# The second products of a batch pair by seven block products, and split weights kept in DRAM

## The chip, the cores and the metric

The kernel runs on one core of a Trainium2 chip. The metric is the time of one execution on the device in microseconds (us), as the median of several runs; a profile is one further execution, recorded instruction by instruction. The engines are TensorE (PE, matrix products), VectorE (DVE), ScalarE (ACT) and GpSimd (POOL); SyncE (SP) issues nearly all transfers.

## What is computed

Four batches of 448 tokens by 768 channels go through attention with 12 heads, a mixer of low rank and a second mixer. Cut to the two mixers, on which the change bears:

```python
# x: (4, 448, 768) from the attention
u = x + ((x.T @ U) @ V).T                      # first mixer, tokens (rank 32)
x = u + relu(u @ wa1) @ wa2                    # "FFN a": 768 -> 3072 -> 768
u = x + (relu(x.T @ w_tok1) @ w_tok2).T        # second mixer, tokens (256)
out = u + relu(u @ wb1) @ wb2                  # "FFN b": 768 -> 1536 -> 768
```

The inputs are float64. A product in full precision is made of three matmuls on values split into a high and a low part: high by high, low by high, high by low.

## The kernel before

**Layout.** Activations lie as channels by tokens: `xs[i]` is a tile of 128 partitions by 6 blocks of 448, one for each batch of a pair. The weights of an FFN are worked in chunks of 128 hidden channels: FFN a has 24, FFN b 12, taken in groups of `G = 2`. Batches 0 and 1 are the first pair, 2 and 3 the second.

**Order of the work.** Attention of batches 0 and 1 comes first (to about 200 us); then FFN a of the first pair runs while the attention of batches 2 and 3 is woven in (to about 620 us), then the first pair's token mixing and FFN b (to about 1000 us), then both FFNs of the second pair in `pair_ffn`.

**Weights.** In the first pair `load_w` loads a chunk (`w_raw`, 768 KB), turns float64 into float32 on ACT, DVE and POOL (`to_f32`), stores the float32 chunk in DRAM (`cache`, tiles `c_a...` and `c_b...`, line 159) and splits it (`split`, lines 143 to 145: high part on ACT, low part on POOL). In the second pair `again` (line 191) loads the cached float32 chunk and splits it once more.

**First products of the second pair.** In the middle groups (10 of FFN a, 4 of FFN b) the first products of both batches and two chunks are a 2 by 2 block product. `seven` (line 615) makes it by seven block products for eight, from weight sums (`w1_blocks`, line 212) and activation sums (`sums`, line 589). A block product is three channel blocks of three matmuls, 9 matmuls of 448 columns: 63 a group.

**Second products.** `second` (line 651) takes, for each batch and each of the six output blocks, two chunks of three matmuls, 12 x 6 = 72 matmuls a group, and DVE adds each output block from PSUM to `xs` (line 659). Those of one group run beside the first products of the next (`rest_`, line 690).

**What sets the order.** The code gives dependencies and a program order; the framework's scheduler puts the instructions of each engine into a fixed order when the program is built. Each engine then works its list in order and waits where a semaphore isn't reached. So does SP: a transfer that waits for its source holds up the transfers behind it. Tiles come from pools with a fixed number of buffers (`wh` and `wl`, the split chunks, have four each; `pu` five).

## Time and profile before

| | us |
|---|---|
| median of 3 runs (lowest, highest) | 1553.95 (1550.92, 1559.37) |
| the profiled execution | 1552.55 |
| its span, first to last instruction | 1550.8 |
| PE busy in the span | 1462.3 (94%) |
| DVE / ACT / POOL busy | 1100.2 / 710.3 / 814.0 |
| mean granted TensorE clock | 0.982 of full speed |

The chain of work that ended last is PE for 69% of the span, DVE for 9%, POOL for 7%, DMA for 6%. In a row of instructions, `out<-in` names the tiles: `ps_g` and `ps_p` are first products (plain and by blocks), `ps_x` second products, `gs` the split hidden activations. Matmuls are pipelined: the time of one row is longer than the distance to the next.

### The profile page before, as it was taken

The page shows a single profiled execution, that of the slowest core. Times are in us where ns is not written, and L with a number is a line of the kernel's source. Part 1 is how long each engine was busy: PE and PEld are TensorE (multiplying, and loading weights), DVE is VectorE, ACT ScalarE, POOL GpSimd, SP SyncE. Part 2 cuts the span into 40 slices and gives each one's busy share as a digit, 9 for nine tenths or more (in the row PEclk, how much of TensorE's full clock was granted, in tenths as well). Part 3 has the DMA queues.
Part 4 walks back from the last instruction along what each step waited for, and adds up shares of the span by engine and source line. Part 5 has one row for each costly group of instructions (what it writes and reads, how often), then busy time and mean ns, then how long its engine had stood idle before and what let it go on. Part 6 is the DMA issues. An engine that isn't in the chain of part 4 may idle for free.

```text
span 1550.8 us, 21621 instructions
## 1 busy us (share of the span) xinstructions
PE 1462.3 (94%) x7522; PEld 1296.6 (84%) x7522; DVE 1100.2 (71%) x1811; ACT 710.3 (46%) x1413; POOL 814.0 (52%) x839
## 2 busy tenths in 40 slices
PE   4999968899999999999899999889999999999998
PEld 3766657788888899898798999779999999998997
DVE  6888877888887888566858766596756655567753
ACT  4777756566566665343634434342322221333311
POOL 6888967777876655454735553024443523103510
PEclk9999979999999999999999999999999999999999
DMA  6756644656655544451505540421211111201203
GB/s 169 171 133 156 175 140 130 182 151 195 194 175 150 147 125 142 165 178 63 194 31 184 183 153 32 157 68 52 72 52 51 62 58 46 77 18 54 72 21 92
DMA packets 96588, 180.94 MB, mean 117 GB/s; under 512 B 8992, under 2 KB 66304, under 8 KB 96480
## 3 DMA queue, kind: packets, MB, share of 16 engines
q1 hardware_dynamic: 96160, 179.57, 37.7%
q8 instruction: 59, 0.97, 0.3%
q14 instruction: 49, 0.40, 0.1%
q10 hardware_dynamic: 320, 0.00, 0.0%
HBM read 107.19 MB, written 36.57 MB: 93 GB/s over the span
## 4 chain that ended last, share of the span: by engine, by line
PE 69%; DVE 9%; POOL 7%; DMA 6%; issue 4%; ACT 3%; SPq 1%; ACTq 0%; DVEq 0%; POOLq 0%
PE ps_x L79 29%; PE ps_g L79 16%; PE ps_p L79 11%; PE pv L79 3%; PE sc L79 2%; PE pt L362 2%; PE ps_u L79 2%; PE ps_t L79 2%; POOL w_bits L134 2%; POOL p L343 1%; DVE w_bits L126 1%; DMA qr<-in_q_dram 1%; POOL w L145 1%; DMA c_a<-w_bits 1%; POOL sq L256 1%
## 5 line engine op out<-in xcount | busy, mean ns | idle before, releaser
L79 PE MATMUL ps_x<-gs,w 128*128 128x448 f32 x2592 | 575.6, 370 | 13.8 <-DVE xT L544 3.9
L79 PEld LDWEIGHTS ps_x<-gs,w 128*128 128x128 f32 x2592 | 484.1, 190 | 58.6 <-DVE xT L544 7.0
L79 PE MATMUL ps_g<-u,w 128*128 128x448 f32 x1584 | 345.0, 370 | 0.9 <-POOL u L445 0.9
L79 PEld LDWEIGHTS ps_g<-u,w 128*128 128x128 f32 x1584 | 296.7, 189 | 25.5 <-POOL u L445 1.2
L134 POOL TENSOR_TENSOR w_bits<-w_bits,w_round 128x768 uint32<-128x768 uint32 (+3 forms) x80 | 143.5, 1794 | 106.6 <-DVE w_bits L131 45.4
L145 POOL TENSOR_TENSOR w<-w 128x768 fp32r<-128x768 f32 x44 | 87.2, 1988 | 196.8 <-ACT w L144 143.3
L145 POOL TENSOR_TENSOR w<-w_bits,w 128x768 fp32r<-128x768 f32 (+3 forms) x82 | 147.6, 1807 | 78.3 <-ACT w L144 74.6
L659 DVE TENSOR_TENSOR xT<-ps_x,xT 128x448 f32<-128x448 f32 x216 | 130.3, 618 | 78.5 <-PE ps_x L79 77.9
L544 DVE TENSOR_TENSOR xT<-ps_x,xT 128x448 f32<-128x448 f32 x216 | 132.3, 616 | 42.1 <-PE ps_x L79 39.2
L336 ACT ACTIVATE p<-sc,nm 112x448 f32<-112x448 f32 x192 | 121.1, 633 | 56.0 <-DVE nm L334 52.7
L343 POOL TENSOR_SCALAR p<-p,sm 112x448 f32<-112x448 f32 x192 | 133.2, 706 | 19.9 <-DVE sm L340 18.0
L79 PE MATMUL sc<-ks,qs 128*112 128x448 f32 x384 | 120.2, 406 | 23.6 <-DMA ks<-both 12.9
L145 POOL TENSOR_TENSOR w_a<-w_a 128x384 fp32r<-128x384 f32 (+1 forms) x28 | 41.2, 1470 | 186.0 <-DVE w_t L223 171.9
L334 DVE TENSOR_REDUCE nm<-sc 112x1 f32<-112x448 f32 x192 | 116.3, 613 | 23.0 <-PE sc L79 21.8
L362 PEld LDWEIGHTS pt<-ident,p 112*112 112x112 f32 x768 | 89.8, 135 | 37.2 <-issue 10.9
L362 PE MATMUL pt<-ident,p 112*112 112x112 f32 x768 | 111.9, 262 | 4.5 <-POOL p L343 3.7
L126 DVE TENSOR_SCALAR w_bits<-w_bits 128x768 f32<-128x768 f32 (+3 forms) x80 | 76.3, 954 | 47.2 <-ACT w_bits L125 46.7
L630 DVE TENSOR_TENSOR pu<-ps_p,pu 128x448 f32<-128x448 f32 x98 | 58.7, 616 | 67.5 <-PE ps_p L79 67.4
L130 ACT ACTIVATE w_round<-w_raw 128x768 uint32<-128x768 uint32 (+3 forms) x80 | 69.8, 873 | 73.4 <-POOL w_bits L134 69.4
L373 ACT ACTIVATE ph<-pt 112x448 fp32r<-112x448 f32 (+1 forms) x168 | 88.4, 543 | 31.1 <-PE pt L362 30.0
L125 ACT ACTIVATE w_bits<-w_raw 128x768 f32<-128x768 f32 (+3 forms) x80 | 70.1, 877 | 55.1 <-POOL w L145 37.3
L377 DVE TENSOR_TENSOR pl<-pt,ph 112x448 fp32r<-112x448 f32 x144 | 87.2, 613 | 10.4 <-ACT ph L373 9.7
(110 smaller groups left out, 2283.9 us busy)
## 6 DMA issues: line engine op xcount, KB each, us to landing
w_raw<-in_moe_w_ch_dram SPq DMA_DIRECT2D x72, 768.0 KB, 4.4
ks<-both SPq DMA_DIRECT2D x92, 224.0 KB, 3.7
c_a<-w_bits SPq DMA_DIRECT2D x48, 384.0 KB, 3.3
qs<-both SPq DMA_DIRECT2D x96, 112.0 KB, 2.9
w<-c_a SPq DMA_DIRECT2D x28, 384.0 KB, 3.2
c_b<-w_bits SPq DMA_DIRECT2D x24, 384.0 KB, 3.2
w_a<-c_a SPq DMA_DIRECT2D x20, 384.0 KB, 2.9
w<-c_b SPq DMA_DIRECT2D x16, 384.0 KB, 3.1
```

What stands on the lines that cost most here:

```text
L79: nc.tensor.matmul(o, lhsT=l, rhs=r, start=start, stop=stop)
L126: nc.vector.tensor_scalar_max(f(w), f(w), TINY)
L134: nc.gpsimd.tensor_tensor(w, w, r, op=ALU.add)
L145: nc.gpsimd.tensor_sub(lo, w, f(hi))
L334: nc.vector.tensor_reduce(nm, sc, axis=AX.X, op=ALU.max, negate=True)
L336: nc.scalar.activation(p, sc, AF.Exp, bias=nm, accum_out=sm[:, c % 2:c % 2 + 1])
L343: nc.gpsimd.tensor_scalar(x, x, sm[:, i:i + 1], 1.0, op0=ALU.mult, op1=ALU.mult)
L362: nc.tensor.transpose(pt[:, c * CP:(c + 1) * CP], pr[c][:, kc * CP:(kc + 1) * CP], ident[:CP, :CP],)
L373: nc.scalar.activation(ph, pt, AF.Copy)
L377: nc.vector.tensor_sub(pl, pt, f(ph))
L544: nc.vector.tensor_add(xT[:, dc], px, xT[:, dc])
L659: nc.vector.tensor_add(xT[:, dc], px, xT[:, dc])
```

## The change

**Split weights in DRAM.** `load_w` now also stores the high and the low part of each chunk (`parts`, tiles `h_a...` and `h_b...`): two more stores of 384 KB for each of the 72 chunks, on SP's queue. `load_wt` stores the split token-mixing weights in eight smaller stores, and `wt_again` loads them back for the second pair. `again` and `halved` load split parts and split nothing.

**Second products by seven.** `second_of` makes a group's second products as seven block products, 7 x 9 = 63 matmuls, each into a trio (one PSUM tile of three banks, two such tiles, shared with the token mixing). The seven sums are kept over all groups of an FFN: in `xs` itself, in the two `raw` buffers and in the `w` and `r` buffers; DVE adds a trio to its sum in one operation of 1344 columns. `join` puts the seven sums together after the last middle group, on DVE and POOL. The hidden activations are now also needed as four sums (`t1` to `t4` in `seven`), each split on ACT and DVE.

**Weight blocks in a ring.** `w1_ring` and `w2_ring` prepare one block for each of the seven rounds, about four rounds ahead: unchanged blocks come split from DRAM, the four sums of each side are made from the cached float32 chunks on POOL and split on ACT and POOL. Ten transfers of 384 KB a group take the place of four. `pu` has 11 buffers, the pool `wt` closes with the first pair.

Per program, PE has 7350 matmuls for 7476; SP issues 800 transfers for 544, POOL 974 instructions for 844.

The diff, cut to its core:

```diff
@@ load_w
+        if keep:
+            parts[keep] = dram.tile([p, 2, n], F32, name=f"h_{keep}")
+            for i, t in enumerate((hi, lo)):
+                nc.sync.dma_start(parts[keep][:, i], f(t))
         return hi, lo
...
     def again(key):
         hi, lo = slots()
-        nc.sync.dma_start(f(lo), cache[key])
-        split(f(lo), hi, lo)
+        for i, t in enumerate((hi, lo)):
+            nc.sync.dma_start(f(t), parts[key][:, i])
         return hi, lo
...
+    def ring(tag, src):
+        t = wp.tile([P, 2, HD], F32R, tag=tag, bufs=4, name="w_b")
+        if len(src.shape) == 3:
+            nc.sync.dma_start(f(t), src)
+        else:
+            split(src, t[:, 0], t[:, 1])
+        return t[:, 0], t[:, 1]
...
+    def w2_ring(nm, j, a):
+        k0, k1 = [f"{nm}2_{j + i}" for i in range(2)]
+        a["a11"] = ring("wl", parts[k0][:, :, :HD])
+        a11, s3, a12, s1 = staged((k0, k1))
+        yield
+        a["a12"] = ring("wl", parts[k1][:, :, :HD])
+        yield
+        add(s1, s3)
+        sub(s3, a11, s3)
+        sub(a11, s1, a11)
+        sub(a12, a12, a11)
+        a["s4"] = ring("wl", a12)
+        yield
+        a["s1"] = ring("wl", s1)
+        yield
+        a["s3"] = ring("wl", s3)
+        yield
+        a["s2"] = ring("wl", a11)
+        yield
+        a["a22"] = ring("wl", parts[k1][:, :, HD:])
+        yield
...
@@ seven
+            def parted(key, t):
+                s = pools["g"].tile([P, 2, S], F32R, tag="g", name="gs")
+                nc.scalar.activation(s[:, 0], t, AF.Copy)
+                nc.vector.tensor_sub(s[:, 1], t, f(s[:, 0]))
+                gs[key] = s[:, 0], s[:, 1]
...
-            gs[1][0] = relu(plus(product("s", "s4", "b22"), u4))
+            g12 = output(None, product("s4", "b22"), u4)
+            t1 = diff(nc.gpsimd, g12, g11)
+            parted("t1", t1)
+            t3 = diff(nc.gpsimd, g22, g12)
+            parted("t3", t3)
+            t2 = diff(nc.vector, g22, t1)
+            parted("t2", t2)
+            parted("t4", diff(nc.vector, g21, t2))
...
+        def second_of(a, gs, acc, fresh):
+            for key, l, r in (("p1", "a11", "b11"), ("p2", "a12", "b21"), ("p3", "s4", "b22"),
+                              ("p5", "s1", "t1"), ("p7", "s3", "t3"), ("p6", "s2", "t2"),
+                              ("p4", "a22", "t4")):
+                px = trio("ps_x")
+                for c in range(HC):
+                    three(px[c], pick(a[l], c), gs[r], True, True)
+                to = acc[key]
+                for x, ps in zip(to, [trios[-1]] if len(to) == 1 else px):
+                    if fresh and key in ("p1", "p5", "p6", "p7"):
+                        nc.scalar.activation(x, ps, AF.Copy)
+                    else:
+                        nc.vector.tensor_add(x, ps, x)
+                yield
+
+        def join(acc):
+            x1, x6, x5 = acc["p1"][0], acc["p6"][0], acc["p5"][0]
+            c11, c12, c21 = [acc[k][0] for k in ("p2", "p3", "p4")]
+            nc.gpsimd.tensor_add(c11, c11, x1)
+            nc.vector.tensor_add(x6, x6, x1)
+            for c, x7 in enumerate(acc["p7"]):
+                nc.vector.tensor_add(x7, x7, x6[:, c])
+                nc.vector.tensor_add(c21[:, c], c21[:, c], x7)
+            nc.gpsimd.tensor_add(c12, c12, x6)
+            nc.gpsimd.tensor_add(c12, c12, x5)
+            x = pools["tb"].tile([P, HC, S], F32, tag="t3", name="x22")
+            nc.sync.dma_start(x, x22)
+            nc.vector.tensor_add(x5, x5, x)
+            for c, x7 in enumerate(acc["p7"]):
+                nc.vector.tensor_add(x5[:, c], x5[:, c], x7)
...
         for j0 in range(G, n - G, G):
-            a = a or w1_blocks(nm, j0)
-            w2s = [w2_chunk(nm, w2, j0 + i) for i in range(G)]
-            gs = [[None] * 2 for _ in xs]
-            for _ in seven(a, b, gs):
-                if j0 > G:
-                    next(rest_, None)
-                    next(rest_, None)
+            more = j0 + G < n - G
+            gs, a2, a_next = {}, {}, {}
+            it = seven(a, b, gs)
+            for r in range(1, 8):
+                for _ in range(1 if j0 > G else 2):
+                    next(rest_, None)
+                next(it)
+                if r == 4:
+                    prep1 = w1_ring(nm, j0 + G, a_next) if more else last_w1()
+                    prep2 = w2_ring(nm, j0, a2)
+                next(prep1, None)
+                next(prep2, None)
...
-    open_pools(rest, (("xs", 4, 0), ("pu", 5, 0), ("tb", 1, 0)))
+    open_pools(rest, (("xs", 4, 0), ("pu", 11, 0), ("tb", 1, 0), ("M", 2, 1), ("p", 2, 1)))
```

**Where instructions stand now.** First the list of PE in the steady loop of FFN a, second pair, one group: `ps_p` are first products by blocks (`w_a`, `w_s`, later `w_b` are weight blocks, `u` and `t_...` activation blocks), `ps_x` second products. Before:

```order
L79 MATMUL ps_p<-u,w_a 128x448 x16
L79 MATMUL ps_p<-t_11161,w_s 128x448 x9
L79 MATMUL ps_x<-gs,w 128x448 x12
L79 MATMUL ps_p<-t_11162,w_a 128x448 x9
L79 MATMUL ps_x<-gs,w 128x448 x12
L79 MATMUL ps_p<-t_11163,w_a 128x448 x9
L79 MATMUL ps_x<-gs,w 128x448 x12
L79 MATMUL ps_p<-t_11258,w_s 128x448 x9
L79 MATMUL ps_x<-gs,w 128x448 x12
L79 MATMUL ps_p<-u,w_s 128x448 x9
```

After, the same place:

```order
L79 MATMUL ps_p<-u,w_b 128x448 x9
L79 MATMUL ps_x<-gs,w_b 128x448 x9
L79 MATMUL ps_p<-t_11392,w_b 128x448 x9
L79 MATMUL ps_x<-gs,w_b 128x448 x9
L79 MATMUL ps_p<-t_11393,w_b 128x448 x9
L79 MATMUL ps_x<-gs,w_b 128x448 x9
L79 MATMUL ps_p<-t_11481,w_b 128x448 x9
L79 MATMUL ps_x<-gs,w_b 128x448 x9
L79 MATMUL ps_p<-t_11394,w_b 128x448 x9
L79 MATMUL ps_x<-gs,w_b 128x448 x9
```

Blocks of nine alternate, where before twelve second products stood between two first ones.

Second, DVE at the turn from one group to the next in the same loop. Before (line 630 adds a first product, 659 a second one, 513 makes the low part of a hidden activation):

```order
L659 TENSOR_TENSOR xT<-ps_x,xT 128x448 x3
L630 TENSOR_TENSOR pu<-ps_p,pu 128x448
L513 SCALAR_TENSOR_TENSOR gs<-pu,gs 128x448
L630 TENSOR_TENSOR pu<-ps_p,pu 128x448
L659 TENSOR_TENSOR xT<-ps_x,xT 128x448 x2
```

After (line 750 adds a first product, 819 a trio, 768 makes a difference of hidden activations, 756 a low part):

```order
L750 TENSOR_TENSOR pu<-ps_p,pu 128x448
L819 TENSOR_TENSOR X<-ps_x,X 128x1344
L768 TENSOR_TENSOR pu<-pu 128x448
L756 TENSOR_TENSOR gs<-pu,gs 128x448
L768 TENSOR_TENSOR pu<-pu 128x448
L756 TENSOR_TENSOR gs<-pu,gs 128x448
L819 TENSOR_TENSOR xT<-ps_x,xT 128x1344
L756 TENSOR_TENSOR gs<-pu,gs 128x448 x2
L750 TENSOR_TENSOR pu<-ps_p,pu 128x448
```

Behind the add of the group's last first product now come six operations on two SBUF tiles, with one add of a trio among them. POOL's list at the same turn, after (line 145 is the low part of a weight block, 264 and 267 the weight sums, 768 the two differences t1 and t3):

```order
L267 TENSOR_TENSOR w_f<-w_f 128x384 x3
L145 TENSOR_TENSOR w_b<-w_f,w_b 128x384 x4
L768 TENSOR_TENSOR pu<-pu 128x448 x2
L145 TENSOR_TENSOR w_b<-w_f,w_b 128x384 x3
L264 TENSOR_TENSOR w_f<-w_f 128x384
```

The differences stand behind four low parts of weight blocks. Third, SP where the first pair's weights begin to be loaded. Before:

```order
L159 DMA c_a_0_2883<-w_bits 128x768
L116 DMA w_raw<-in_moe_w_ch_dram 128x6x128
L116 DMA w_raw<-in_moe_w_ch_dram 128x768 x2
L159 DMA c_a_1_2899<-w_bits 128x768
L116 DMA w_raw<-in_moe_w_ch_dram 128x6x128
L159 DMA c_a_0_3176<-w_bits 128x768
```

After:

```order
L159 DMA c_a_0_2883<-w_bits 128x768
L169 DMA h_a_0_2889<-w 128x768 x2
L116 DMA w_raw<-in_moe_w_ch_dram 128x6x128
L116 DMA w_raw<-in_moe_w_ch_dram 128x768 x2
L159 DMA c_a_1_2902<-w_bits 128x768
L169 DMA h_a_1_2908<-w 128x768
L116 DMA w_raw<-in_moe_w_ch_dram 128x6x128
L169 DMA h_a_1_2908<-w 128x768
L159 DMA c_a_0_3182<-w_bits 128x768
```

The stores of the high and the low part stand in front of the next chunks' loads.

## Rows read from the trace of the kernel before

**Rows 1.** Busy time by stage; window, its length, then each engine's busy us.

```profile
core 0: us, PE busy (x) PEld busy (x) DVE busy (x) ACT busy (x) POOL busy (x), PEclk, DMA share, GB/s
0.00:200.00 200.00, 162.64 (x886) 119.73 (x886) 155.99 (x318) 134.43 (x361) 160.96 (x303) 0.96 0.64 158
200.00:620.00 420.00, 397.47 (x2127) 352.79 (x2128) 343.32 (x572) 260.47 (x532) 294.62 (x313) 0.97 0.52 159
620.00:930.00 310.00, 297.37 (x1474) 270.21 (x1473) 215.37 (x299) 133.25 (x194) 162.65 (x95) 0.99 0.41 144
930.00:1050.00 120.00, 111.36 (x568) 98.43 (x567) 85.93 (x141) 45.05 (x86) 32.54 (x22) 0.99 0.25 84
1127.09:1281.82 154.73, 154.73 (x765) 143.37 (x765) 93.27 (x150) 40.99 (x70) 60.53 (x43) 1.00 0.17 57
1281.82:1401.90 120.08, 118.32 (x605) 108.85 (x604) 70.11 (x119) 39.38 (x73) 26.34 (x16) 0.99 0.14 48
...
1495.60:1550.80 55.20, 49.59 (x264) 45.23 (x262) 23.36 (x38) 9.51 (x17) 7.71 (x4) 0.98 0.23 70
```

**Rows 2.** Chain that ended last, steady loop; start us, length us, what.

```profile
1127.09 5.07 PE ps_p L79 x25
...
1149.38 2.44 PE ps_x L79 x12
...
1154.45 5.07 PE ps_p L79 x25
```

**Rows 3.** Instruction groups of DVE, 1127 to 1282 us; count, busy us, mean ns, idle before.

```profile
L659 DVE TENSOR_TENSOR xT<-ps_x,xT 128x448 f32<-128x448 f32 x67 | 41.5, 621 | 23.1 <-PE ps_x L79 23.0
L630 DVE TENSOR_TENSOR pu<-ps_p,pu 128x448 f32<-128x448 f32 x39 | 23.7, 617 | 30.6 <-PE ps_p L79 30.6
L513 DVE SCALAR_TENSOR_TENSOR gs<-pu,gs 128x448 fp32r<-128x448 f32 x22 | 17.6, 800 | 4.7 <-ACT gs L512 4.4
```

**Rows 4.** Instruction groups of DVE, 930 to 1127 us, 384 columns from PSUM.

```profile
L439 DVE TENSOR_TENSOR xs<-pt_x,xs 112x384 fp32r<-112x384 f32 x16 | 8.4, 550 | 3.5 <-ACT xs L438 3.4
```

**Rows 5.** Instruction groups of POOL, 1127 to 1282 us.

```profile
L145 POOL TENSOR_TENSOR w_a<-w_a 128x768 fp32r<-128x768 f32 x5 | 9.3, 1854 | 0.0
...
L145 POOL TENSOR_TENSOR w_a<-w_t,w_a 128x384 fp32r<-128x384 f32 x5 | 5.1, 1020 | 5.3 <-ACT w_a L144 5.3
```

**Rows 6.** Timelines of POOL and DVE; start us, length us, instruction.

```profile
1150.47 1.86 POOL L145 TENSOR_TENSOR w_a<-w_a 128x768 fp32r<-128x768 f32 x1
1152.28 2.23 POOL L145 TENSOR_TENSOR w<-w 128x768 fp32r<-128x768 f32 x1
...
1151.40 1.41 DVE L513 SCALAR_TENSOR_TENSOR gs<-pu,gs 128x448 fp32r<-128x448 f32 x1
```

**Rows 7.** One line's instructions over the run; duration ns lowest/median/highest.

```profile
L513 DVE SCALAR_TENSOR_TENSOR gs<-pu,gs x56: 606/626/2179, 1032.4 to 1497.4; 128x448 fp32r<-128x448 f32 x56
```

**Rows 8.** Who PE waited for, 930 us to the end; us, times, longest.

```profile
PE ps_p L79 <- DVE t L598: 2.3, 4, 1.0
PE ps_x L79 <- DVE xT L659: 2.1, 2, 1.7
PE ps_x L79 <- ACT w L144: 1.3, 1, 1.3
```

**Rows 9.** Transfers, 200 to 930 us: queue's packets, MB, share; issues, median us to landing.

```profile
q1 hardware_dynamic: 58537, 110.47, 47.2%
...
c_a<-w_bits SPq DMA_DIRECT2D x48, 384.0 KB, 3.3
```

**Rows 10.** Who ACT waited for, 200 to 930 us.

```profile
ACT both L300 <- DMA qs<-both: 16.3, 7, 5.6
...
ACT w_bits L125 <- DMA c_a<-w_bits: 5.9, 4, 2.3
```

**Rows 11.** Chain that ended last, 200 to 930 us, shares by line.

```profile
by line: PE ps_g L79 25.4%; PE ps_x L79 24.4%; issue 5.0%; PE sc L79 3.7%; PE pt L362 3.4%; PE pv L79 3.3%; POOL w_bits L134 3.3%; DVE w_bits L126 2.7%; POOL w L145 2.6%; DMA c_a<-w_bits 2.5%; DVE w_bits L131 2.0%; PE ps_u L79 1.8%; DVE w_b
```

More of the change, by code (lines that the diff above doesn't have):

```diff
@@ new lines, in w1_blocks, with w1_ring @@
+        sub(a12, a12, a11)
+        split(a12, *res["s4"])
+        return res
+    def ring(tag, src):
[5 more added lines that the diff above has]
+        return t[:, 0], t[:, 1]
+    def w1_ring(nm, j, a):
+        k0, k1 = [f"{nm}1_{j + i}" for i in range(2)]
+        a["a11"] = ring("wh", parts[k0][:, :, :HD])
+        a11, a12, s3, s1 = staged((k0, k1))
+        yield
+        a["a12"] = ring("wh", parts[k0][:, :, HD:])
+        yield
+        add(s1, s3)
+        sub(s3, a11, s3)
+        sub(a11, s1, a11)
+        a["s2"] = ring("wh", a11)
+        yield
+        a["s3"] = ring("wh", s3)
+        yield
+        a["s1"] = ring("wh", s1)
+        yield
+        a["a22"] = ring("wh", parts[k1][:, :, HD:])
+        yield
+        sub(a12, a12, a11)
+        a["s4"] = ring("wh", a12)
+        yield
@@ L474, in rank_steps, with trio @@
             yield
+    trios = []
+    def trio(name):
+        t = pools["M"].tile([P, 3, 512], F32, tag="M", name=name)
+        trios.append(t[:, :, :S])
+        return [t[:, i, :S] for i in range(3)]
     def token_mix(xT, w):
@@ L479, in token_mix @@
         for hf in range(2):
-            pts = [psum("ts"[rc], [P, HALF], "ps_t1") for rc in range(RC)]
+            if trios:
+                pts = [t[:, :HALF] for t in trio("ps_t1")]
+            else:
+                pts = [psum("ts"[rc], [P, HALF], "ps_t1") for rc in range(RC)]
             for c, (xh, xl) in enumerate(to_tokens(xT, hf)):
@@ L573, in ffn, with pair_ffn @@
                         after(i)
-    def pair_ffn(nm, w1, w2, xs, us, a, after, half=None, last=lambda: None, begun=None):
+    def pair_ffn(nm, w1, w2, xs, us, a, after, half=None, last=lambda: None, begun=None,
+                 late=lambda: None):
         n = w1.shape[1] // P
@@ L660, in second @@
-                if done and dc % 3 == 2:
-                    done(dc // 3)
-                yield
-        def seconds(gs, w2s):
-            for xT, g in zip(xs, gs):
-                yield from second(xT, g, w2s)
-        def chunks(j0):
-            return ([w1_chunk(nm, w1, j0 + i) for i in range(G)],
-                    [w2_chunk(nm, w2, j0 + i) for i in range(G)])
+                if dc % 3 == 0:
+                    px = trio("ps_x")
+                for i, (g, w) in enumerate(zip(gs, ws)):
+                    three(px[dc % 3], pick(w, dc), g, i == 0, i == len(gs) - 1)
@@ L698, in pair_ffn, with last_w1 @@
-        drain(rest_)
-        for i in range(2):
-            drain(second(xs[i], [first(us[i], ws) for ws in w1s], w2s,
-                         half and (lambda h: half(i, h))))
-            after(i)
+        prep1, prep2 = iter(()), iter(())
+        x22 = dram.tile([P, HC, S], F32, name=f"x22_{nm}")
+        acc, w1s = None, []
+        def last_w1():
+            for i in range(n - G, n):
+                key, res = f"{nm}1_{i}", []
+                w1s.append(res)
+                for h in range(2):
+                    res.append(ring("wh", parts[key][:, :, h * HD:(h + 1) * HD]))
+                    yield
@@ new lines, in pair_ffn @@
+        w = late()
+        w2s = []
+        gs = []
+        for r in range(1, 8):
+            next(rest_)
+            next(prep2, None)
+            if r in (2, 4):
+                gs.append(first(us[0], w1s[len(gs)]))
+            if r > 3:
+                i = r - 4
+                if i % 2 == 0:
+                    w2s.append([])
+                key = f"{nm}2_{n - G + i // 2}"
+                w2s[-1].append(ring("wl", parts[key][:, :, (i % 2) * HD:(i % 2 + 1) * HD]))
+        join(acc)
@@ L704, in begin @@
+        for i in range(2):
+            if i:
+                gs = [first(us[1], ws) for ws in w1s]
+                last()
+            drain(second(xs[i], gs, w2s, half and (lambda h: half(i, h))))
+            after(i, w)
     def begin(nm, w1, u, beside=iter(())):
```

206 lines of the change are left out of this document (138 added, 68 removed).

## The prediction, made before the changed kernel was run

> **What bounds the kernel now.** I read the profile by stages first. The table of stages [rows 1] gives for each stretch how long PE was busy and at which granted clock. Before 200 us PE idles a fifth of the time (attention alone). From 200 to 930 us, the first pair of batches, it idles 22.5 + 12.6 = 35 us. From 930 us on, the second pair, it idles only 8.6 + 1.8 + 5.6 = 16 us, and in the steady loop of the second pair PE has no gap at all, at clock 1.00. The reader should see that DVE, at 93 of 155 us there, and POOL, at 61, have room. Then I read the chain of waits [rows 2]: in the loop it is one unbroken line of matmuls, and a group of two chunks repeats every 1154.45 - 1127.09 = 27.36 us. A group has 63 first-product matmuls and 72 second-product ones, so one costs 27.36 / 135 = 0.2027 us; the rows of 12 (2.44 us) say the same. So in the second pair, time is the number of matmuls, as long as the other engines keep up. Third I read what the other engines need per instruction in the loop [rows 3 to 7], and last what is queued in the first pair [rows 9 to 11], since the change adds stores there.
>
> **What is removed.** Each of the 14 groups (10 in FFN a, 4 in FFN b) goes from 72 second-product matmuls to 7 x 9 = 63. That is 126 fewer (the built program has 7350 matmuls for 7476), all on the chain: 126 x 0.2027 = **25.5 us**. A group then needs 126 x 0.2027 = 25.54 us of PE. Everything else in the change can only add, or return part of the 16 us of idle time.
>
> **The loop: does DVE keep up?** I count a group's DVE work after the change. Sums of a product in PSUM with one SBUF operand: 7 `plus` at 0.617 us [rows 3] are 4.3 us. Six adds of three banks at once (1344 columns): from 384 columns at 550 ns [rows 4] to 448 at 617 ns a column costs 1.03 ns, so 617 + 896 x 1.03 ns = 1.54 us each, an estimate, 9.2 us together. The seventh sum goes in three pieces, 1.9 us. Then nine operations with both inputs in SBUF (seven low parts in `parted`, two differences), 0.62 us each when alone, 5.6 us. Sum 21.0 of 25.54 us. Before, DVE had about 16.5 us in 27.36 [rows 1].
>
> Those nine are the weak point. The timeline shows an operation with two SBUF inputs taking twice its time or more when POOL is at work: 1.41 us instead of about 0.62 while POOL's 1.86 us subtraction ended, and POOL's next one then took 2.23 us instead of 1.85 [rows 6]. Over the run the low parts of line 513 range from 606 to 2179 ns [rows 7]. The adds from PSUM in the same stretch do not lengthen; their means stay at 621 and 617 ns [rows 3]. So a two-SBUF operation waits for the POOL operation in flight, and POOL's next for it. The change takes DVE's four weight sums away, but gives POOL per group eight sums and eight low parts of 384 columns and two differences of 448. At 1.02 us for 384 and 1.85 us for 768 columns [rows 5] a column costs 2.2 ns, so 448 cost 1.16 us: 16 x 1.02 + 2 x 1.16 = 18.6 us of 25.54, against about 11 before. If one of the nine meets POOL busy 73% of the time and waits half an operation, it waits 0.37 us: 3.3 us more, DVE at 24.3 us. POOL, held in return for about nine times 0.5 us, is at 23.1. Both fit into 25.54, with 5 and 10% to spare.
>
> The Trainium skill ("SBUF — State Buffer", section "SBUF: two separate sides") calls this an exclusive lock that either engine keeps for its whole instruction, and not a sharing of bandwidth. The trace agrees, by the 1.41 us above. By that rule alone the 18.6 and the 5.6 us could never overlap, which is the first rival.
>
> At the turn of a group six of the nine stand together. The new order has them behind one another on DVE (the difference t2, the low part of t1, t4, the low parts of t3, t2 and t4) with one add of three banks between them, while the PE queue runs on. Put the end of the last first product at 0. PE has six blocks of nine (10.9 us) before it needs the second of the two PSUM trios again. DVE finishes the p1 sum at 3.4 us; four of the six, each behind a POOL operation, take 4 x 1.4 = 5.6 us; the sum that frees the trio ends near 10.5. It just fits. The next release of a product bank, behind the last two, comes near 13.4 against 12.8 needed. So I expect a stall of some tenths per turn: 0.4 us x 13 turns = **+5 us**, with ends at 0 (POOL idle at the turn) and +24 (the whole gain of a group).
>
> Weights in the loop: ten transfers of 384 KB a group instead of four, 3.9 MB in 25.5 us or about 154 GB/s, which stretches of the first pair already carry (159 GB/s, [rows 1]). They are asked for three to four rounds of 3.65 us ahead and land in about 3 us [rows 9]; I count them at nothing. Without that lead each would cost up to 3 us.
>
> **The first pair.** 144 stores of 384 KB and eight small ones are added on SP's queue between 200 and 930 us: 111 + 58 = 169 MB, so the share of the DMA engines goes from 47 to at most 72% [rows 9]. Each low-part store waits on SP for POOL's subtraction; queued behind it are the next `w_raw` load and the attention's `qs` and `ks` copies. Who waits for those: ACT, 16.3 us for `qs`, 5.9 us for the `c_a` stores [rows 10]; PE never on a transfer after 200 us. Half as much again of the 22 us is 11 us of ACT; ACT has 160 of 420 us free there and PE 22, so I let a third through: **+4 us**, ends -2 (the scheduler's order shifts a little) and +12.
>
> **Ends and starts of the second pair.** The two joins add about 9 us of DVE work each (twice 1.54, nine times 0.62) and 9 us of POOL's (three times 1344 columns at 2.2 ns) after the last products, while PE has the 36 matmuls of the last chunk's second products (7.3 us), then the token mixing, whose three-bank PSUM tiles now share two trios with `ps_x`. I take +1.5 us at each, **+3 us**, ends 0 and +8. At the starts the weights come split from DRAM, so ACT and POOL no longer work ahead of them, and `pu` has 11 buffers for 5. The waits that this can return are DVE's t sums, DVE's xT and ACT's w, 2.3 + 2.1 + 1.3 us [rows 8]: **-2 us**, ends -4 and +2.
>
> **Sum.** The profiled execution took 1552.55 us (span 1550.8), 1.4 us under the median of 1553.95, well inside that kernel's spread, so I make no correction: 1552.55 - 25.5 + 5 + 4 + 3 - 2 = **1537 us**.
>
> **Rivals.**
> 1. DVE becomes the bound through POOL. The period is the larger of 25.54 and 21.0 + 9w, w the wait of one of the nine. It decides from w = 0.50 us; a full POOL operation (1.02) would give 30.2, which POOL's own idle time forbids in the long run. At w = 0.65 the group takes 26.9, the loop costs 13 x 1.3 = 17 instead of 5: **1549 us**. For it: six in a row, each behind a POOL operation. Against it: the waits of a DVE that is late leave POOL without work.
> 2. Slower: the stores in the first pair. In the stretch from 200 to 930 us the chain holds 2.5% of 730 us, 18 us, of landing `c_a` stores [rows 11]. Store bytes triple (384 to 1152 KB a chunk). Were the chain held three times as long, that is +37 instead of +4: **1570 us**. It ends above the time before once the first pair loses more than 20 us. Against it: the high and low parts have four buffers each and are not on the way to PE, unlike the `c_a` source, which has two.
> 3. All covers hold: no stall at the turns, nothing lost in the first pair, all 4 us back at the starts: 1552.55 - 25.5 + 0 + 0 + 3 - 4 = **1526 us**.
>
> **Chances.** Forecast 0.55 (1530 to 1545), rival 1 0.17, rival 2 0.08, rival 3 0.20. What a measurement of this kernel can tell from no change is about 0.5% or 7.8 us, so faster means under 1546.2 and slower over 1561.7. Faster: 0.55 + 0.20 + 0.02 of rival 1 = 0.77; same: the rest of rival 1 less a little, 0.14; slower: rival 2 and the far end of rival 1, 0.09. The range reaches from rival 3 with a little more (1521, the floor if every small end falls well) to the far side of rival 1 (1556).
>
> **What would show it.** Right: `ps_p` and `ps_x` alternate in nines, the group period lies between 25.5 and 26.3 us, PE's gaps in the loop stand only at the turns and end on a DVE sum; DVE's two-SBUF operations average 0.9 to 1.1 us; the first pair ends within 10 us of 930. Wrong: a period of 26.9 or more with PE waiting for DVE in most rounds (rival 1); the first pair ending 20 us or more later with ACT waiting for `qs` or `c_a` (rival 2); PE waiting for a weight block's transfer or its split, which I counted at nothing; more than 5 us lost at a join.

## The result, and the profile after

| | before | after |
|---|---|---|
| median of 6 runs each, same chip (us) | 1557.91 | 1575.38 |
| ratio, 95% interval | | 1.011 (1.0075 to 1.0145) |
| the profiled execution / its span (us) | 1552.55 / 1550.8 | 1574.69 / 1572.9 |
| PE / DVE / ACT / POOL busy (us) | 1462.3 / 1100.2 / 710.3 / 814.0 | 1451.4 / 1185.8 / 744.6 / 937.0 |

The change makes the kernel slower by 1.1%. The forecast was 1537 us, with 1521 to 1556 as the range. The reader should first see in which stage the 22.1 us of span went. I cut both traces at the same places of the program: the end of the fourth long block of second products in the first pair's FFN b, the end of the last first-product block of FFN a, and that of FFN b in the second pair. The table of stages (from:to, length, busy time of PE, of its weight loads, of DVE, ACT and POOL with instruction counts, granted clock, DMA share, GB/s) of the kernel before, cut there:

```profile
200.00:933.54 733.54, 698.38 (x3616) 626.28 (x3617) 561.85 (x875) 395.82 (x731) 459.13 (x409) 0.98 0.48 152
933.54:1285.82 352.28, 343.64 (x1714) 313.66 (x1712) 230.79 (x369) 108.75 (x195) 128.33 (x89) 1.00 0.20 67
1285.82:1495.39 209.57, 207.81 (x1045) 191.55 (x1044) 128.18 (x213) 61.79 (x111) 57.88 (x37) 0.99 0.14 48
1495.39:1550.80 55.41, 49.80 (x265) 45.42 (x263) 23.37 (x38) 9.51 (x17) 7.71 (x4) 0.98 0.23 71
```

And of the changed kernel (it answers to [rows 1]):

```profile
200.00:946.28 746.28, 705.27 (x3662) 631.85 (x3663) 567.89 (x890) 400.89 (x742) 465.03 (x414) 0.98 0.69 229
946.28:1283.12 336.84, 323.10 (x1586) 292.05 (x1585) 260.15 (x316) 127.48 (x249) 201.83 (x172) 0.99 0.47 150
1283.12:1504.45 221.33, 206.28 (x1010) 185.80 (x1008) 160.41 (x197) 73.84 (x142) 95.89 (x76) 0.98 0.36 113
1504.45:1572.90 68.45, 53.55 (x256) 44.93 (x254) 42.50 (x52) 9.70 (x19) 14.86 (x8) 0.94 0.26 75
```

The stages change by +12.7, -15.4, +11.8 and +13.0 us, which is the 22.1. At 0.2027 us each the removed matmuls should have given 0, -16.4 (81), -7.3 (36) and -1.8 us (9). One more correction: the scheduler now does the first mixer of batch 2 inside the first stage. Its matmuls (16 `ps_h`, 18 `pt_x`, 12 `ps_u`, about 7 us by the distances of their rows) stood behind the cut before and stand ahead of it now:

```profile
933.54 0.34 PE L79 MATMUL ps_h<-xs,w 112*128 112x384 f32 x1
```

```profile
810.36 0.34 PE L79 MATMUL ps_h<-xs,w 112*128 112x384 f32 x1
```

With that, the losses against a kernel that only lost 126 matmuls are about 6 us in the first pair, 8 at the start and in the loop of FFN a, 19.1 from its end through FFN b, and 14.8 at the end: together 47.6 us against a gain of 25.5. About 4 of the 8 us in FFN a are not the change's (last section).

**The loop does what it should.** In FFN a, blocks of nine alternate without a gap (PE's timeline; start, length, row), and between 1064 and 1283 us PE waits for nothing:

```profile
1152.92 2.02 PE L79 MATMUL ps_x<-gs,w_b 128*128 128x448 f32 x9
1154.78 2.02 PE L79 MATMUL ps_p<-u,w_b 128*128 128x448 f32 x9
```

DVE's and POOL's groups in the loop of the changed kernel (count, busy us, mean ns, idle before) answer to [rows 3] and [rows 5]:

```profile
L819 DVE TENSOR_TENSOR xT<-ps_x,xT 128x1344 f32<-128x1344 f32 x32 | 49.5, 1548 | 6.1 <-PE ps_x L79 6.1
L756 DVE TENSOR_TENSOR gs<-pu,gs 128x448 fp32r<-128x448 f32 x57 | 46.6, 828 | 2.7 <-ACT gs L755 2.7
L768 DVE TENSOR_TENSOR pu<-pu 128x448 f32<-128x448 f32 x16 | 23.5, 1471 | 0.9 <-POOL pu L768 0.5
...
L768 POOL TENSOR_TENSOR pu<-pu 128x448 f32<-128x448 f32 x16 | 18.2, 1157 | 0.9 <-ACT pu L761 0.9
```

**The ends of the loop do not.** Whom PE waited for from 946 us on (total, times, longest), beside [rows 8], where the largest sum was 2.3 us:

```profile
PE ps_x L79 <- ACT gs L755: 6.3, 1, 6.3
PE ps_x L79 <- DVE xT L847: 5.6, 2, 5.1
PE ps_x L79 <- DVE xT L819: 5.2, 3, 2.7
PE ps_x L79 <- DVE xT L852: 3.9, 2, 3.3
PE ps_t L79 <- DVE xs L544: 3.2, 2, 2.6
...
PE ps_x L79 <- DMA w_b<-h_a: 1.0, 1, 1.0
PE ps_x L79 <- DMA w_b<-h_b: 1.0, 1, 1.0
```

The first stands at the start of FFN a (1033 us), the second at the last join (1530), the third and fourth at the starts of both FFNs, the fifth in the token mixing behind the first join, and the two waits for a weight block's transfer at the two joins. Around these gaps the granted clock falls: it is 0.86 in all three stretches of 25 us, where the kernel before had 1.00 in the middle one (second fence). The 0.86 is a mean of two levels: from 1036.1 to 1042.9 us, for example, the granted clock is 0.50, the lower level (1.2 GHz).

```profile
1025.00:1050.00 25.00, 17.92 (x79) 15.83 (x78) 16.36 (x20) 8.73 (x16) 16.43 (x14) 0.86 0.14 44
1300.00:1325.00 25.00, 18.82 (x89) 16.10 (x88) 22.17 (x22) 1.85 (x4) 6.44 (x2) 0.86 0.30 98
1525.00:1550.00 25.00, 16.58 (x72) 12.66 (x71) 18.33 (x22) 1.96 (x4) 6.37 (x2) 0.86 0.27 79
...
1036.10:1042.90 6.80, 3.52 (x9) 3.14 (x10) 2.35 (x3) 3.20 (x7) 4.64 (x4) 0.50 0.29 74
```

```profile
1300.00:1325.00 25.00, 25.00 (x130) 23.15 (x129) 7.44 (x14) 5.82 (x10) 5.48 (x3) 1.00 0.20 64
```

### The profile page after: what moved, and what is told of

It is laid out like the page before. It is cut to its first block, busy times and chain, and to the rows that moved or that the text cites. A ratio compares the mean times of both kernels' runs of the same rounds, so it can differ in the third digit from the quotient of the medians.

```text
span 1572.9 us, 22129 instructions
## 1 busy us (share of the span) xinstructions
PE 1451.4 (92%) x7396; PEld 1274.1 (81%) x7396; DVE 1185.8 (75%) x1769; ACT 744.6 (47%) x1507; POOL 937.0 (60%) x969
## 4 chain that ended last, share of the span: by engine, by line
PE 58%; DVE 13%; DMA 9%; POOL 8%; ACT 5%; issue 5%; SPq 1%; ACTq 0%; POOLq 0%; DVEq 0%
PE ps_x L79 24%; PE ps_g L79 13%; PE ps_p L79 10%; PE sc L79 3%; PE pv L79 2%; PE pt L467 2%; DVE w_bits L126 2%; DVE w_bits L131 2%; DVE w_bits L127 2%; PE ps_u L79 1%; POOL p L448 1%; PE ps_t L79 1%; DMA ks<-both 1%; DMA w_raw<-in_moe_w_ch_dram 1%; POOL w L145 1%
## 5 line engine op out<-in xcount | busy, mean ns | idle before, releaser
L79 PE MATMUL ps_x<-gs,w 128*128 128x448 f32 x1440 | 326.6, 372 | 19.0 <-DVE xT L660 7.0
L79 PE MATMUL ps_g<-u,w 128*128 128x448 f32 x1440 | 310.7, 369 | 2.0 <-DVE gs L630 1.5
L79 PEld LDWEIGHTS ps_x<-gs,w 128*128 128x128 f32 x1440 | 267.6, 190 | 45.4 <-DVE xT L660 10.1
L79 PEld LDWEIGHTS ps_g<-u,w 128*128 128x128 f32 x1440 | 267.9, 188 | 26.3 <-DVE gs L630 2.1
L79 PE MATMUL ps_x<-gs,w_b 128*128 128x448 f32 x1026 | 232.6, 371 | 19.7 <-ACT gs L755 6.3
L79 PEld LDWEIGHTS ps_x<-gs,w_b 128*128 128x128 f32 x1026 | 193.1, 190 | 41.3 <-issue 8.3
L660 DVE TENSOR_TENSOR xT<-ps_x,xT 128x448 f32<-128x448 f32 x216 | 132.8, 619 | 42.7 <-PE ps_x L79 40.7
L145 POOL TENSOR_TENSOR w_b<-w_f,w_b 128x384 fp32r<-128x384 f32 x104 | 118.4, 1153 | 66.2 <-ACT w_b L144 65.6
L264 POOL TENSOR_TENSOR w_f<-w_f 128x384 f32<-128x384 f32 x28 | 45.3, 1619 | 174.0 <-DMA w_f<-c_b 67.7
L79 PE MATMUL sc<-ks,qs 128*112 128x448 f32 x384 | 119.9, 406 | 22.1 <-DMA ks<-both 11.7
L761 ACT ACTIVATE pu<-pu 128x448 f32<-128x448 f32 x56 | 32.3, 577 | 136.1 <-DVE pu L750 135.5
```

What stands on the lines that cost most here:

```text
L79: nc.tensor.matmul(o, lhsT=l, rhs=r, start=start, stop=stop)
L145: nc.gpsimd.tensor_sub(lo, w, f(hi))
L660: nc.vector.tensor_add(xT[:, dc], px, xT[:, dc])
```

## The experiments

My theory after the result: the loop gains its 25 us, and they go (A) to the joins, (B) to the starts of the two FFNs, both through DVE and POOL shutting one another out, and (C) to the stores in the first pair. Ratios below are to the kernel before on the same chip; the changed kernel's is 1.011.

**The stores alone.** The kernel before with `load_w` and `load_wt` storing the split parts, which nobody reads, once whole and once with 16 columns of each:

```diff
+        if keep:
+            parts[keep] = dram.tile([p, 2, n], F32, name=f"h_{keep}")
+            for i, t in enumerate((hi, lo)):
+                nc.sync.dma_start(parts[keep][:, i], f(t))            # e1_stores
+                nc.sync.dma_start(parts[keep][:, i, :16], f(t[:, :16]))  # e2_tiny
```

> The kernel before with nothing added but the stores: high and low part of each of the 72 weight chunks and the split token-mixing weights go to DRAM, and nobody reads them. In the changed kernel the middle of the first pair's FFN b is reached 12.7 us later than before. Theory A, the stores alone cost that: the same point (933.5 us before) comes at 942 to 948 us, and the whole is 10 to 14 us longer than the kernel before (1.006 to 1.009). Rival B, the loss comes from the rest of the change (other pools, another order): the point stays within 4 us of 933.5 and the ratio within 0.997 to 1.003.

> As the kernel with the stores alone, with as many stores in the same places, waiting for the same instructions, but each of 16 columns (8 KB) in place of 768 (384 KB); nobody reads them. If it is bytes that cost (the DMA engines' share of 0.69 against 0.47, loads landing later), the loss is gone: the mid of FFN b within 4 us of 933.5 us. If it is SP's queue (174 us of waits of stores for ACT and POOL, with loads queued behind them), the loss stays: 940 to 948 us and 1.005 to 1.009 in the whole.

Measured: 1564.03 us, 1.005 (1.0025 to 1.0075), with the whole stores, 1558.50 us, 1.0026 (1.0006 to 1.0046), with the small ones. The long block of second products before the cut, kernel with whole stores, with small ones, and before:

```profile
928.12 15.04 PE L79 MATMUL ps_x<-gs,w 128*128 128x448 f32 x72
```

```profile
919.23 14.75 PE L79 MATMUL ps_x<-gs,w 128*128 128x448 f32 x72
```

```profile
918.96 14.75 PE L79 MATMUL ps_x<-gs,w 128*128 128x448 f32 x72
```

The block ends at 943.2 us with the stores, at 934.0 with small ones, at 933.7 before. These are single executions, so their spread matters. Counted from the first product of FFN a (212.8, 211.7 and 214.2 us), the block ends after 730.4, 722.3 and 719.5 us; in the changed kernel and the seven below that keep its whole first pair, the same stretch takes 732.0 to 736.2 us, a spread of 4.2. The 8 us between whole and small stores (some 1.5 of them by the slower pace of the last section, at which the first block above ran) are outside such a spread, the 2.8 us between small stores and none are not. So in the traces it is mostly bytes, not the order on SP's queue: as many stores with the same waits cost little there. The ratios of the runs don't part the two, since their intervals overlap; that of the small stores alone, some 4 us, is above zero, and what it consists of is open (their profiled execution, one of the quickest of its twelve, shows no later stage). On the whole, the stores cost less than the 10 to 14 us expected. What the bytes do is seen in the landing times (issues, KB, median us from issue to landing) of the kernel with whole stores and of that with small ones; [rows 9] has 3.3 for `c_a`:

```profile
w_raw<-in_moe_w_ch_dram SPq DMA_DIRECT2D x72, 768.0 KB, 5.4
...
c_a<-w_bits SPq DMA_DIRECT2D x48, 384.0 KB, 4.9
```

```profile
w_raw<-in_moe_w_ch_dram SPq DMA_DIRECT2D x72, 768.0 KB, 4.5
...
c_a<-w_bits SPq DMA_DIRECT2D x48, 384.0 KB, 3.6
```

**The joins left out.**

```diff
-        join(acc)
         for i in range(2):
```

> The changed kernel with the join of the seven sums left out in both FFNs of the second pair (the sums are not put together, so that part of the computation is missing). Theory A, the join costs 10 to 13 us at each place (PE waits of 2.3, 2.6 and 5.1 us and the lower granted clock behind them): 1549 to 1556 us against 1575. Rival B, the ends cost mainly because the second products, the token mixing and the transposes now share two PSUM trios and one pool of two banks: the waits stay and only 2 to 7 us come back, 1568 to 1573 us.

Measured: 1564.72 us, 1.0073 (1.0047 to 1.0099). In the profile the last two stages together take 276.4 us for 289.8. So the joins as such cost 13.4 us there, two fifths of the 33.9 that the two stages lose. By the ratios it is some 6 us, and there the intervals overlap. What stays stands at the start of FFN b (3.3 us), one group later (2.9) and in the token mixing. The time lies between theory A (1549 to 1556) and rival B (1568 to 1573): the joins are not the whole of it. Whether the rest comes from the shared PSUM trios, as rival B has it, this run doesn't tell.

**The join in another order, first try.**

```diff
-            for c, x7 in enumerate(acc["p7"]): ...   # x7 += x6; c21 += x7
-            nc.gpsimd.tensor_add(c12, c12, x6)
-            nc.gpsimd.tensor_add(c12, c12, x5)
+            nc.vector.tensor_add(c12, c12, x6)
+            nc.vector.tensor_add(c12, c12, x5)
+            yield                                    # rest behind batch 2's second products
+            for c, x7 in enumerate(acc["p7"]): ...
```

> The changed kernel with the same join in another order: the two long additions of 1344 columns that batch 2 waits for go from POOL to DVE, at the head, and DVE's nine additions for batch 3 are written behind batch 2's second products, so that no DVE instruction with two inputs in SBUF stands beside a long one of POOL. Theory A, the price of the join is DVE standing behind POOL (three additions of 448 columns took 6.24 us for 1.9): most of it comes back, 6 to 10 us at each join, 1556 to 1564 us. Rival B, the price is the amount of work on DVE: DVE gets 3.1 us more of it at each join, and 1573 to 1580 us come out.

Measured: 1566.97 us, 1.0087 (1.0055 to 1.0119), between the two expectations. I had mistaken `c12` for a quarter of batch 2; it belongs to batch 3, and batch 2 misses its three `c21` additions here. What the run still shows is the price of POOL. In the changed kernel three additions of 448 columns on DVE took 6.24 us beside POOL's long ones:

```profile
1306.45 6.24 DVE L830 TENSOR_TENSOR X<-X,X 128x448 f32<-128x448 f32 x3
...
1305.15 3.09 POOL L832 TENSOR_TENSOR xT<-xT,X 128x1344 f32<-128x1344 f32 x1 [9.59 <-DVE X L828]
1308.32 3.35 POOL L833 TENSOR_TENSOR xT<-xT 128x1344 f32<-128x1344 f32 x1
```

Without POOL beside them the same three took 1.69 us:

```profile
1302.86 1.69 DVE L833 TENSOR_TENSOR X<-X,X 128x448 f32<-128x448 f32 x3
```

Batch 2 waits for DVE's additions, and they stood behind POOL's additions for batch 3, which nobody needed yet.

**The order put right, and batch 3's first products ahead of the join**, each alone and both together:

```diff
             for c, x7 in enumerate(acc["p7"]): ...   # as before, first
+            yield
-            nc.gpsimd.tensor_add(c12, c12, x6)
-            nc.gpsimd.tensor_add(c12, c12, x5)
+            nc.vector.tensor_add(c12, c12, x6)       # behind batch 2's second products
+            nc.vector.tensor_add(c12, c12, x5)
```

```diff
             if r in (2, 4):
                 gs.append(first(us[0], w1s[len(gs)]))
+            if r in (5, 7):
+                gs.append(first(us[1], w1s[len(gs) - 2]))
```

> The changed kernel with the join in another order, nothing left out. (In the kernel e4_join I had taken c21 for a quarter of batch 3; it is batch 2's, so that there batch 2 missed three of its additions, which came too late.) Here DVE makes x6, x7 and c21, which batch 2 waits for, first; the two long additions to c12, which only batch 3 needs, go from POOL to DVE and are written behind batch 2's second products. Theory A, the price of the join is that DVE's six small additions stand behind POOL's two long ones (6.24 us for three of them): the waits of 2.3, 2.6 and 5.1 us shrink by more than half and 4 to 9 us come back over both joins, 1566 to 1571 us against 1575. Rival B, the price is the chain itself (last sum, x6, x7, c21, second products, transposes), whatever POOL does: less than 3 us come back.

> The changed kernel with batch 3's first products of the last two chunks (36 matmuls, 7.3 us) written ahead of the join, so that they stand in PE's queue before batch 2's second products. Theory A, the join is a chain of waits that other PE work can cover: PE's waits for the join (2.3, 2.6, 5.1 us) shrink by the 7.3 us at each, and 6 to 12 us come back, 1563 to 1569 us. Rival B, the same matmuls are then missing beside the token mixing and the last transposes: the gaps come up there, and the time stays within 3 us of 1575.

> The changed kernel with the two edits at the joins together and nothing else: join in the other order, batch 3's first products ahead of the join. One alone gave 1574.44 (order) and 1572.04 us (first products), 1 and 3 us; the kernel with all edits gave 1552.46. Theory A, the two need one another (the order makes the chain shorter, the products cover what is left), and the joins are most of what the change lost: 9 to 14 us of 1575 come back, 1561 to 1566 us, 1.003 to 1.007 of the kernel before. Rival B, what the last kernel gained came from the starts and the stores: at most 5 us come back, 1.008 to 1.012.

Measured: order alone 1574.44 us, 1.0133 (1.0106 to 1.0159); products alone 1572.04, 1.0128 (1.0102 to 1.0153); both 1566.49, 1.0074 (1.0049 to 1.0098). Alone neither tells itself from the changed kernel, as the two rivals had it. Together they give back about 6 us by the ratios, at the edge between what the theory and the rival expected; their interval overlaps the changed kernel's, but lies below those of both single edits. The profile says why: with the products alone PE still waits 4.9 us for DVE at the last join; with both, the waits there are 1.86, 0.83 and 1.34 us, and the last two stages take 277.4 us for 289.8:

```profile
1275.90:1492.74 216.84, 206.25 (x1009) 185.55 (x1008) 157.09 (x199) 74.64 (x142) 89.59 (x74) 0.98 0.37 117
1492.74:1553.30 60.56, 49.70 (x256) 43.37 (x254) 40.42 (x54) 9.84 (x19) 8.09 (x6) 0.99 0.30 85
```

The three kernels below that hold both edits (e9_all, e11_all2, e12_one) take 276.4 to 277.8 us for these stages, the kernel without any join 276.4, and the kernels with one edit 286.1 and 290.5. So the profiles agree that the two edits take back all that the joins cost, 12 to 13 us; the runs show about half of it.

**The starts.** Early weight sums on POOL, and in another kernel the first group's weight sums and low parts on DVE:

```diff
         kept = keep_first()
+        pre2, pre1 = w2_sums(nm, G), w1_sums(nm, 2 * G)   # e6_early: staged, add, sub as in the rings
```

```diff
+                on[0] = nc.vector if j0 == G else nc.gpsimd    # e10_dve: add, sub, split's low part
                 next(prep1, None)
                 next(prep2, None)
+                on[0] = nc.gpsimd
```

> The changed kernel with the weight sums of the first middle group of each FFN (and of the group after it) made on POOL before the activation sums are written, not during them. In the changed kernel POOL's first such addition took 7.88 us for 1.02 (7.24 in FFN b), while DVE ran its sums back to back; ACT's queue stood 9.45 us behind POOL's weight sums, and PE 6.3 us behind ACT. Theory A, that is the price of the start: POOL's first additions take about 1 us each, PE's wait of 6.3 us near 1035 us is gone, and 5 to 9 us come back in all, 1566 to 1570 us. Rival B, the start is bound by DVE's own sums: the wait only goes over to DVE and at most 2 us come back.

> The changed kernel with the weight sums and the low parts of the first middle group of each FFN made on DVE in place of POOL (384 columns: about 0.55 us for 1.02). In the kernel with early sums POOL's additions took 1.0 to 1.4 us each, but then DVE came late and PE waited 5.68 us for it: the start's time only changed hands. Theory A, at a start DVE and POOL exclude one another, and what counts is the sum of their two-input work: about 8 x 0.47 us less of it, so that PE's wait near 1035 us falls from 6.3 to 2 to 4 us and 4 to 8 us of 1575 come back over both starts. Rival B, DVE's own queue is the bound, and 4.4 us more work on it make the start longer: 1577 to 1583 us.

Measured: early 1581.63 us, 1.0172 (1.0143 to 1.0202); on DVE 1573.85, 1.0114 (1.007 to 1.0158). The early sums weren't early: their first addition starts at 1019 us, as before. They gave nothing back; the time is some 10 us above the changed kernel's by the ratios, and the cause of that stays open. But this trace shows the other face of the start. In the changed kernel POOL's first addition stands 7.88 us, ACT waits 9.45 us behind it, and PE 6.31 us for ACT:

```profile
1019.50 7.88 POOL L264 TENSOR_TENSOR w_f<-w_f 128x384 f32<-128x384 f32 x1 [67.09 <-PE ps_p L79]
...
1036.03 1.76 ACT L144 ACTIVATE w_b<-w_f 128x384 fp32r<-128x384 f32 x4 [9.45 <-POOL w_f L267]
...
1039.38 1.11 PE L79 MATMUL ps_x<-gs,w_b 128*128 128x448 f32 x2 [6.31 <-ACT gs L755]
```

Meanwhile DVE makes its activation sums back to back, one each 0.53 us:

```profile
1019.98 0.62 DVE L725 TENSOR_TENSOR pu<-xT 128x448 f32<-128x448 f32 x1
1020.52 0.62 DVE L726 TENSOR_TENSOR pu<-t,t 128x448 f32<-128x448 f32 x1
```

In the kernel with the early sums POOL gets in first and takes 1.01 to 1.4 us each; now DVE's sums come one each 1.36 us:

```profile
1019.19 1.01 POOL L264 TENSOR_TENSOR w_f<-w_f 128x384 f32<-128x384 f32 x1 [67.80 <-DMA w_f<-c_a]
...
1021.97 1.44 DVE L745 TENSOR_TENSOR pu<-t,t 128x448 f32<-128x448 f32 x1
1023.32 1.43 DVE L744 TENSOR_TENSOR pu<-xT 128x448 f32<-128x448 f32 x1
```

and PE waits for DVE instead, by nearly as much (whom PE waited for, from 960 us):

```profile
PE ps_p L79 <- DVE pu L769: 5.7, 1, 5.7
```

Five other kernels run here have the start's old code (e3_nojoin, e4_join, e5_join2, e8_fill, e13_ends); in all five PE waits 5.7 us for DVE at FFN a, and in four of them POOL's first addition at FFN b stands over 7 us. So the other face isn't the work of the early sums; the old code shows it more often than the first one. PE loses nearly the same at FFN a either way, which fits a start that costs the sum of what both engines have to do; and nothing came back, as the rival had it. The long wait at the start of FFN b is another matter. There POOL's addition stood 7.24 us, so that DVE kept its full pace, and the addition that PE waited 3.3 us for (it frees one of the two trios) still came late, behind DVE's own row of activation sums:

```profile
1395.53 7.24 POOL L264 TENSOR_TENSOR w_f<-w_f 128x384 f32<-128x384 f32 x1 [10.96 <-DVE pu L726]
...
1401.82 1.56 DVE L852 TENSOR_TENSOR xT<-ps_x,xT 128x1344 f32<-128x1344 f32 x1
```

Where POOL got in there (e5_join2, e6_early) this wait is 4.6 us. On DVE the same additions take 0.547 us for 1.02, and the wait near 1035 us falls to two of 2.3 us together; but the one in the next group grew from 2.2 to 3.5 us, the one at FFN b from 3.3 to 3.8, and alone the edit gives nothing that can be measured; the time lies between the two expectations:

```profile
L269 DVE TENSOR_TENSOR w_f<-w_f 128x384 f32<-128x384 f32 x5 | 2.7, 547 | 0.0
```

**All together.** The two edits at the joins, 17 MB fewer stores, and at the start first the early sums, then DVE in their place:

```diff
+            o, e = 0, n                              # weight parts that nobody reads
+            if mid and keep[1] == "1" and j % 2: o = HD
+            if mid and keep[1] == "2" and j % 2 == 0: e = HD
             for i, t in enumerate((hi, lo)):
-                nc.sync.dma_start(parts[keep][:, i], f(t))
+                nc.sync.dma_start(parts[keep][:, i, o:e], f(t[:, o:e]))
```

> The three edits together (join in the other order, early weight sums, batch 3's first products ahead of the join), and 17 MB fewer stores in the first pair (weight parts and float32 chunks that nobody reads are not stored). If the loss of the change stands at the joins, the starts and the stores, as the profile has it, 18 to 28 us of 1575 come back: 1547 to 1557 us, 0.990 to 0.998 of the kernel before. If these places only pass their waits on to one another, it stays above 1562 us.

> The kernel e9_all with this edit in place of the early sums: join in the other order, batch 3's first products ahead of the join, fewer stores, first group's weight sums on DVE. If the parts add up: e9_all (1.0078 of the kernel before) less 4 to 8 us, 1.003 to 1.005. If the starts are bound by DVE's own queue: 1.008 or more.

Measured: with the early sums 1565.63 us, 1.0078 (1.005 to 1.0106), above what I expected; with DVE 1552.46 us, 0.9988 (0.9965 to 1.0011), below the 1.003 to 1.005 that the parts add up to. The second takes back what the change lost, some 19 us by the ratios, and stands level with the kernel before. The two differ only in the start; but as the early sums seemed to cost time of their own, their difference is not the price of POOL's sums alone. Against e13_ends (1.0074), which has the old start and all the stores, the second gains nearly as much as against the first. Whom PE waited for from 960 us on, in the second:

```profile
PE ps_x L79 <- DVE xT L865: 4.2, 2, 3.8
PE ps_p L79 <- DVE pu L761: 3.8, 3, 1.7
```

**And without the stores.**

```diff
+            if parts:
+                parts[keep] = parts["a1_0"]          # only the first chunk's parts are stored
+                return hi, lo
```

> The kernel e11_all2 with the parts of only one weight chunk stored in the first pair; the second pair loads this one chunk's parts in every place (so its unchanged weight blocks are not the right ones), as many bytes as before. It shows what the change is worth with its stores at nothing. Theory A, the stores cost 9 to 13 us (the kernel before lost 9.6 us by them at the middle of FFN b): 9 to 13 us under e11_all2, 0.994 to 0.998 of the kernel before. Rival B, what is lost in the first pair is slack that the second pair gives back: within 4 us of e11_all2.

Measured: 1548.04 us, 0.9947 (0.9923 to 0.997), 6.4 us under the kernel with stores by the ratios; `w_raw` lands in 4.5 us again. That lies between the theory (9 to 13) and the rival (within 4); together with the 7.8 us of the stores on the kernel before, some 6 to 8 us is what the runs support, each with an interval of several us.

## Why the prediction was wrong

- **Removed matmuls, 25.5 us: right.** PE ran the expected 126 fewer, and the loop of FFN b repeats every 25.5 us. In FFN a it was 26.0, not by a wait: each matmul took 2% longer in this execution (last section).
- **The turns of the loop, +5 (0 to 24): too dear.** No PE wait stands between 1064 and 1283 us. The prices were right: the nine operations on two SBUF tiles took 0.96 us on the mean (57 low parts at 0.83, 16 differences at 1.47), inside the 0.9 to 1.1 I had named; the operation of three banks 1.55 for the estimated 1.54 (rows 4 and 3 give 1.05 ns a column, not 1.03, and with it 1.55); POOL's 448 columns 1.16 as estimated. What failed is the step from these prices to a stall at each turn. Rival 1 did not happen.
- **The first pair, +4 (-2 to 12): somewhat small, inside its ends.** About 6 us in the profile, 6 to 8 by the runs. The mechanism was probably taken wrongly: I argued mostly with what waits behind the stores on SP's queue, and the kernel with small stores shows little loss by the queue in that stage; with the whole ones the transfers land later. That the later landings are what holds PE up is argued, not shown wait by wait. Rival 2 was this at five times its size.
- **The joins, +3 (0 to 8): the first step that failed.** I had the operations right (9 us of DVE, 9 of POOL) and took PE's 36 matmuls and the mixing as cover. But the additions for batch 2 stood on DVE behind POOL's for batch 3, at 6.24 us for three, and PE's queue had batch 2's second products and its transposes next, not batch 3's products. At the last join PE idled 5.1 us at once, the stage lost 14.8 us (60% of it idle time, the rest behind a granted clock of 0.94). Leaving the joins out, or mending them by both edits, gives back 12 to 13 us of the profile for the 3 of the forecast. I had weighed the shutting out in the loop alone, where it found slack.
- **The starts, -2 (-4 to +2): the second, with the wrong sign.** I counted what ACT and POOL no longer do there and forgot what they do instead: eight weight sums on POOL now fall into DVE's row of activation sums, which has no slack. PE's wait of 6.3 us at FFN a is the result (5.7 us in other executions, then for DVE), and the runs bear it out once the joins are repaired: with these sums on DVE 0.9988, with early sums on POOL 1.0078. PE's 3.3 us at FFN b are not: they come while POOL stands, and stay with the sums on DVE (3.8). They end on the addition that frees a trio.
- **What I had counted at nothing.** Of the 33.9 us lost behind FFN a's last first-product block, the joins make 12 to 13. Some 21 us stay in every changed kernel here, with both edits or without a join, in the token mixing, at the start of FFN b and behind its loop. The forecast had named the trios shared with the token mixing there and left them no price of their own. Which part of the change makes this loss is not shown.
- Of what I had named as signs against me, two came true: more than 5 us lost at a join, and PE waiting for a weight block's transfer, 1.0 us at each join.

The Trainium skill ("SBUF — State Buffer", section "SBUF: two separate sides") says that whichever of DVE (with two SBUF inputs) and GpSimd starts first keeps the shared ports for its whole instruction. The traces agree at all three places: DVE's additions from PSUM keep 0.61 us beside POOL, the ones from SBUF don't. By the rule alone the start costs the sum of both engines' work, and the two faces of the start of FFN a (6.3 and 5.7 us) fit that. That DVE can hold POOL off for many instructions on end stands in the traces only.

What stays open: how the remaining loss in the kernel without stores splits. It is 8 us faster than the kernel before, not 25.5; its PE waits from 960 us on, mixing and the start of FFN b above all, and the clock behind them were seen but not taken away one by one. The obvious suspect, two PSUM trios that now serve second products, mixing and transposes alike, was named as a rival and never tested by itself.

## What to carry to other kernels

When a loop is made denser, cost its first and last turn instruction by instruction, as the loop itself: there the engines that fill the slack of the loop (here DVE and POOL, which shut one another out) meet the work that has none. Ask of each of these instructions for whom it is and what stands in the bound engine's queue meanwhile; here the two edits at the joins gave little alone and 6 us (runs) to 12 us (profiles) together, since one shortens the chain and the other covers it. And gains of a few per cent are spent quickly: about a quarter of the 25 us went to 56 MB of stores (111 to 167 MB between 200 and 930 us) that looked hidden.

## What the runs showed of the hardware

**DVE can starve POOL.** An addition of 384 columns that takes 1.02 us alone stood 7.88 us (7.24 at FFN b) while DVE issued two-input operations back to back at its own full pace. In other executions POOL got in between the same operations; then both alternated, 1.36 us a pair, and DVE was the late one. Which of the two it is seems to hang on who is first at the start; the price to PE was 6.3 or 5.7 us at FFN a. There are seven such standing additions in the traces, one at FFN a and six at FFN b, and each ended 0.94 to 0.97 us after DVE began its next addition with one input from PSUM (at 1402.77 us, behind the start at 1401.82, in the rows above). So in all seven POOL got in with the first operation behind DVE's row that had no two inputs in SBUF.

**The same matmul at two paces under one granted clock.** In 180 us of the loop of FFN a (stages, 1100 to 1280 us), the kernel before, the same loop with stores in the first pair, the changed kernel, and the one with repaired joins:

```profile
1100.00:1280.00 180.00, 180.00 (x890) 166.80 (x889) 108.97 (x176) 47.94 (x82) 71.02 (x50) 1.00 0.17 58
```

```profile
1100.00:1280.00 180.00, 180.00 (x873) 163.50 (x872) 111.63 (x175) 50.55 (x87) 80.33 (x56) 1.00 0.18 58
```

```profile
1100.00:1280.00 180.00, 180.00 (x872) 163.52 (x871) 158.46 (x175) 69.47 (x138) 137.53 (x123) 1.00 0.50 158
```

```profile
1100.00:1280.00 180.00, 179.87 (x888) 166.17 (x887) 160.79 (x177) 69.09 (x139) 136.82 (x123) 1.00 0.53 167
```

PE is busy throughout, the clock reads 1.00 in all four, and yet 890 and 888 matmuls ran in two of them, 873 and 872 in the others, whichever the loop was: 0.2027 and 0.2067 us each. In one execution either pace holds over hundreds of us. It makes some 4 us in the changed kernel's profile that are not the change's, and goes some way to explain why single executions of one kernel lie 10 us apart. What sets the pace, these runs don't show.
